# First terms copied into PSUM by ScalarE, and seven block products in one more down projection

## The chip, the cores and the metric

The kernel runs on one core of one Trainium2 chip. The metric is the device time of one launch in microseconds (us); the kernel before takes 1612.51 us as the median of three runs (1612.45 to 1613.25). One further execution was recorded by the hardware profiler, and every row shown is from that one. The engines are named as in the profile: PE is TensorE (its weight loads are PEld), DVE is VectorE, ACT is ScalarE, POOL is GpSimd, SP is SyncE, which here only issues DMAs. An engine works off its own queue in order. A matmul writes to one of eight PSUM banks of 128x512 fp32.

## The reference

Four layers work on an activation `x` of 2048 rows by 512 columns, with fp32 inputs and results. Layers 0 and 2 are Fourier mixings, layers 1 and 3 are GEGLU blocks; the two kinds share their weights:

```
z = layernorm(x)
mixing:  x = x + Cs @ (z @ Cd^T) - Ss @ (z @ Sd^T)          Cs, Ss 2048x2048; Cd, Sd 512x512
geglu:   x = x + (gelu(z @ w_gate) * (z @ w_up)) @ w_down    1792 hidden columns
```

## The kernel before, in words

**Three products for one.** Every fp32 operand is held as two tiles, a rounded part and the remainder (`split`, lines 145 to 149: ACT copies the rounded part, DVE subtracts it). `mm3` (lines 194 to 198) then makes one fp32 product of three matmuls over 512 columns, two with the rounded part of the left operand and one with its remainder.

**Seven products for eight.** Most large products are cut into two by two blocks, and seven block products are made in place of eight. Their operands are sums and differences of blocks, S1 to S4 on one side and T1 to T4 on the other; some block products share first terms, so that a sum that one of them left behind is added to the next.

**A mixing** works on four blocks `b` of 512 output rows. Its plan (lines 398 to 407) is: stage A11 for all four blocks, stage A12 for all four, and then for each block S2 (three interleaved sums: T2, T1 and T3), two groups of hidden products, S4, four groups, and two last groups. A11 leaves two tiles `sums[b]`, copied out of PSUM by ACT. A12 adds its own two banks to them on DVE (line 790) and puts `sums[b]` and the new sum away in HBM for blocks 1 to 3. S2 fetches both again; when the T2 banks are done, DVE adds `sums[b]` to them (`based`, line 753), and when T1 and T3 are done, DVE adds those too. The hidden products of a block collect in four banks over all eight groups, and at the end DVE adds the old rows of `x` to each bank (`x_add`, line 236) and POOL's queue writes them to HBM.

**A GEGLU layer** works on two halves `w` of 1024 rows. `up(n)`, n from 0 to 13, makes the gate and up products as seven block products; A11's result is copied out by ACT, and DVE adds A12's bank to it (`second`, line 1017). The down projection is of one of two kinds, by the table `SEVEN`. In its plain form (`down_steps`) 14 tiles of `w_down` are multiplied into four banks for each of two row parts. With an entry in `SEVEN`, pairs of tiles are multiplied as block products (`down_product`), half of them beside `up` and the rest behind it. Before the change three of the four GEGLU halves have an entry; the first half of layer 1 is plain.

**Who orders the work.** The program is written in order, and a scheduler of the language then places each instruction on its engine's queue by its own estimate of times. Two things bind it: `behind` (line 140), by which an instruction is not placed on its engine ahead of the last one there that read a PSUM bank (`bank_read`), from the S2 stage of the first mixing and throughout the second; and the pools of SBUF slots (94 tiles of 2 KB per partition) and PSUM banks, given out first in, first out. `queue` holds steps that are run one by one after a product, `slow` holds steps run at every ninth.

**The down projection's block pieces.** `weight_steps` (line 882) loads a pair of `w_down` tiles (three DMAs of 256, 128 and 128 KB), makes four half-width sums on DVE, splits four tiles and writes seven tiles of 256 KB to HBM through POOL's queue. In the kernel before, the seven pairs are made during `up` of the second half of layer 1.

Of the kernel before, what the change touches and what calls it, by code (L numbers as in the profile page):

```python
# [32 lines left out]
PACE = 9  # L33
SKEW = 2, 1
NSLOT = 94
SEVEN = {(1, 1): 7, (3, 0): 7, (3, 1): 5}
FORE = {0: 4, 2: 4}
MADE = 5
LEAD = 3
NK = NS // 2  # L40


@with_exitstack
def fnet_geglu(ctx: ExitStack, tc: tile.TileContext, x_in, ws, wh, wgu, wdn, wdc, out):
# [144 lines left out]
    def copied(src):  # L189
        v = sb.get()  # L190
        bank_read["ACT"] = nc.scalar.activation(v, src, AF.Copy)  # L191
        return v

    def mm3(ps, a, b, start, stop):
        (ah, al), (bh, bl) = a, b
        nc.tensor.matmul(ps, ah, bh, start=start, stop=False, skip_group_check=True)  # L196
        nc.tensor.matmul(ps, ah, bl, start=False, stop=False, skip_group_check=True)  # L197
        nc.tensor.matmul(ps, al, bh, start=False, stop=stop, skip_group_check=True)  # L198
# [46 lines left out]


    away = {}

# [230 lines left out]
    queue, slow, steps_done = [], [], [0]  # L479

    def step():
# [4 lines left out]
        steps_done[0] += 1  # L486
        if slow and steps_done[0] % PACE == 0:
            slow.pop(0)()
# [214 lines left out]
    def mix(layer):  # L703
# [14 lines left out]
        def hid_groups(b, groups):  # L718
# [9 lines left out]
            if last:  # L728
                xrows = [x_load(layer, b * NT + i) for i in range(NT)]
            for n, g in enumerate(groups):  # L730
                (hi, lo), w = take()
                for i in range(NT):
                    ts = slice(i * P, (i + 1) * P)
                    mm3(hid[b][i], (hi[:, ts], lo[:, ts]), w, first and n == 0, last and n == len(groups) - 1)
                sb.put(hi, lo, *w)
# [4 lines left out]
            if last:  # L740
                for i, ps in enumerate(hid.pop(b)):
                    x_add(layer, b * NT + i, xrows[i], ps)

# [8 lines left out]

        def based(b, c, ps):

            if b >= FORE[layer]:
                return copied(ps)
            v = sb.get()
            plus(v, sums[b][c], ps)
            return v

        def a11(b):
# [10 lines left out]
            sums[b] = [copied(p) for p in chain]  # L772
            if b < FORE[layer]:
                ps8.put(*chain)
            else:
                chains[b] = chain

        def a12(b):
            stream["more"] = 0
            if layer and b == 0:  # L780
                lend("x")
                lend("z")
            side = [ps8.get() for _ in range(2)]
            for k in range(NK):
                six(side, "B21", k, k == 0, k == NK - 1, "21" if b == NB - 1 else None)
            for c in range(2):
                v = sums[b][c]
                if b < FORE[layer]:
                    t = sb.get()
                    plus(t, v, side[c])  # L790
                    if b:
                        put_away((layer, b, c), v)
                        put_away((layer, b, c, "sum"), t)
                    else:
                        cs[0, c] = t
                else:
                    plus(v, v, side[c])
                    cs[0, c] = v
            ps8.put(*side)

        chains, sides, us, later = {}, {}, {}, {}

        def s2(b):
            last, fore = b == NB - 1, b < FORE[layer]
            if b == 0:
                lend("z")
                lend("x")
            if fore:
                chains[b] = [ps8.get() for _ in range(2)]
                if b:  # L810
                    sums[b] = [fetched((layer, b, c)) for c in range(2)]
                    cs.update({(0, c): fetched((layer, b, c, "sum")) for c in range(2)})
            chain, one, three = chains.pop(b), [ps8.get() for _ in range(2)], [ps8.get() for _ in range(2)]
            sides[b] = one, three
            if last:
                queue.extend([None] * 14 + [run for fetch in later.pop("fetches") for run in (None, fetch)])
            for i, k in skewed(3):
                if i == 0:
                    six(chain, "T2", k, fore and k == 0, k == NK - 1)
                elif i == 1:  # L820
# [5 lines left out]
                if i == 0:  # L826
                    us[b] = [based(b, c, p) for c, p in enumerate(chain)]
                    ps8.put(*chain)
                    if fore:
                        sb.put(*sums.pop(b))  # L830
                for c in range(2):
# [29 lines left out]
        for n, (b, what) in enumerate(plan(layer)):  # L861
            if n == len(plan(layer)) - 1:
# [10 lines left out]
        in_order[0] = False  # L873


# [48 lines left out]
    def down_weight_steps(k):  # L924
        return weight_steps(k, wdc, wdd)

    down_making = {}

# [26 lines left out]
    def geglu(w, layer):  # L955
# [55 lines left out]
        def first(n):  # L1011
            if n < NF:
                chain[n] = ps8.get()
                product(n, chain[n], "A11", "B11", True, True)
                c11[n] = copied(chain[n])

        def second(n):
            if n < NF:
                ps = ps8.get()
# [4 lines left out]
                finished(n, 0, 0, v)  # L1024
                sb.put(v)

        def up(n):
            if layer == 1 and w == 1:
                k, odd = divmod(n + 3, 2)
                if not odd and 2 <= k < NP:  # L1030
                    down_making[k] = down_weight_steps(k)
                    down_making[k][0]()
                if n % 2 == 0 and n // 2 + 1 in down_making:
                    queue.extend(down_making.pop(n // 2 + 1)[1])
            if n + 3 in making:
# [222 lines left out]
        if w == 0:  # L1258
            norms, others = block_steps(layer, 1)
            slow.extend(norms)  # L1260
            ahead_of_all = others[:ND] if layer in (3,) else []
        if not plain_down and layer == 1 or layer == 3:
# [18 lines left out]
        if w == 0:  # L1281
            queue.extend(([None] * 4 if ahead_of_all else []) + others[len(ahead_of_all):])
            if layer == 1:
                down_making.update((k, down_weight_steps(k)) for k in range(2))
                queue.extend([down_making[0][0], down_making[1][0], *down_making.pop(0)[1]])
        elif before_mix:
# [156 lines left out]
```

## Time and profile before

| what | value |
|---|---|
| median of three runs | 1612.51 us |
| span of the profiled execution, first to last instruction | 1611.3 us |
| what lies between the two | 1.2 us |
| PE busy | 1604.3 us (100%), 7050 matmul records |
| DVE, ACT, POOL busy | 1173.5, 819.9, 272.9 us |
| DMA | 424.67 MB, mean 264 GB/s |
| granted TensorE clock | 1.000 |

The profile's page counts for each engine how long it was busy, and follows one chain of waits back from the last instruction. A row of instructions names the line of the kernel, the engine, the operation, the tile written and the tiles read (s is an SBUF slot, p a PSUM bank, xwide and wide are slots lent from a larger tile, wb and wc are weight pieces in HBM), the shapes and the count; then the busy time, the mean duration of one, and the engine's idle time ahead of them with what ended it. Successive matmuls overlap, so the mean of 389 ns is one matmul's duration and not the distance between two.

### The profile page before, as it was taken

The page shows a single profiled execution, that of the slowest core. Times are in us where ns is not written, and L with a number is a line of the kernel's source. Part 1 is how long each engine was busy: PE and PEld are TensorE (multiplying, and loading weights), DVE is VectorE, ACT ScalarE, POOL GpSimd, SP SyncE. Part 2 cuts the span into 40 slices and gives each one's busy share as a digit, 9 for nine tenths or more (in the row PEclk, how much of TensorE's full clock was granted, in tenths as well). Part 3 has the DMA queues.
Part 4 walks back from the last instruction along what each step waited for, and adds up shares of the span by engine and source line. Part 5 has one row for each costly group of instructions (what it writes and reads, how often), then busy time and mean ns, then how long its engine had stood idle before and what let it go on. Part 6 is the DMA issues. An engine that isn't in the chain of part 4 may idle for free.

```text
span 1611.3 us, 22744 instructions
## 1 busy us (share of the span) xinstructions
PE 1604.3 (100%) x7050; PEld 1322.7 (82%) x7050; DVE 1173.5 (73%) x2025; ACT 819.9 (51%) x1566; POOL 272.9 (17%) x497
## 2 busy tenths in 40 slices
PE   9999999999999999999999999999999999999999
PEld 6888888888888888888888888888888888788887
DVE  7997888789867565666879978887864558844574
ACT  8744363535766434555756433644445535433360
POOL 4111010242545113220031000110400000010001
PEclk9999999999999999999999999999999999999999
DMA  9767786899978799986895776968989777796455
GB/s 358 266 232 256 248 304 220 281 304 326 348 274 297 223 351 322 369 297 231 283 304 184 245 256 196 318 210 307 274 280 276 244 218 217 233 301 203 148 179 157
DMA packets 250090, 424.67 MB, mean 264 GB/s; under 512 B 28848, under 2 KB 90032, under 8 KB 248944
## 3 DMA queue, kind: packets, MB, share of 16 engines
q1 hardware_dynamic: 223488, 334.33, 64.9%
q0 software_dynamic: 26480, 88.89, 15.2%
q8 instruction: 56, 0.92, 0.2%
q14 instruction: 66, 0.54, 0.1%
HBM read 339.48 MB, written 83.62 MB: 263 GB/s over the span
## 4 chain that ended last, share of the span: by engine, by line
PE 97%; DMA 1%; DVE 0%; POOL 0%; ACT 0%; issue 0%; SPq 0%; DVEq 0%; ACTq 0%; POOLq 0%
PE p L196 32%; PE p L197 32%; PE p L198 32%; DMA s<-wb 0%; DMA s<-t 0%; DMA s<-x 0%; DMA s<-ws 0%; DVE s L149 0%; DVE s L180 0%; ACT s L147 0%; POOL rstd L519 0%; SPq L224 0%; ACT s L556 0%; SPq L294 0%; POOL s L652 0%
## 5 line engine op out<-in xcount | busy, mean ns | idle before, releaser
L197 PE MATMUL p<-s,s 128*128 128x512 f32 x2334 | 905.7, 389 | 0.0
L198 PE MATMUL p<-s,s 128*128 128x512 f32 x2334 | 897.1, 389 | 0.0
L196 PE MATMUL p<-s,s 128*128 128x512 f32 x2334 | 866.6, 389 | 1.8 <-DMA s<-wb 1.3
L147 ACT ACTIVATE s<-s 128x512 fp32r<-128x512 f32 (+1 forms) x787 | 447.6, 606 | 333.9 <-PE p L198 59.0
L149 DVE TENSOR_TENSOR s<-s,s 128x512 fp32r<-128x512 f32 (+1 forms) x787 | 494.6, 662 | 93.6 <-ACT s L147 76.4
L196 PEld LDWEIGHTS p<-s,s 128*128 128x128 f32 x2334 | 437.9, 188 | 94.1 <-DMA s<-wb 1.7
L197 PEld LDWEIGHTS p<-s,s 128*128 128x128 f32 x2334 | 438.0, 188 | 92.2 <-DVE s L149 1.1
L198 PEld LDWEIGHTS p<-s,s 128*128 128x128 f32 x2334 | 438.1, 188 | 91.0
L184 DVE TENSOR_TENSOR s<-s,p 128x512 f32<-128x512 f32 x286 | 192.9, 683 | 212.8 <-PE p L198 124.9
L191 ACT ACTIVATE s<-p 128x512 f32<-128x512 f32 x218 | 127.9, 592 | 139.0 <-PE p L198 133.9
L180 DVE TENSOR_TENSOR s<-s,s 128x512 f32<-128x512 f32 (+1 forms) x323 | 193.3, 614 | 1.3
L952 ACT ACTIVATE s<-s 128x512 f32<-128x512 f32 x103 | 64.7, 629 | 74.9 <-DVE s L184 72.5
L147 ACT ACTIVATE s<-xwide 128x512 fp32r<-128x512 f32 x83 | 50.9, 622 | 68.0 <-PE p L197 17.6
L533 POOL TENSOR_SCALAR rstd<-rstd 128x1 f32<-128x1 f32 x40 | 20.5, 512 | 342.3 <-ACT s L532 335.9
L149 DVE TENSOR_TENSOR s<-xwide,s 128x512 fp32r<-128x512 f32 x83 | 56.4, 684 | 22.4 <-ACT s L147 22.0
L278 POOL DMA_DIRECT2D wb<-s x84 | 45.6, 545 | 57.1 <-ACT s L147 45.0
L530 ACT ACTIVATE s<-s 128x512 f32<-128x512 f32 x33 | 20.8, 629 | 67.6 <-PE p L198 32.8
L966 DVE TENSOR_TENSOR s<-s,s 128x512 f32<-128x512 f32 x75 | 51.7, 689 | 1.8
L556 ACT ACTIVATE s<-s,shift,rstd 128x512 f32<-128x512 f32 x56 | 45.3, 811 | 14.4 <-DVE shift L523 8.9
L187 DVE TENSOR_TENSOR s<-s,s 128x512 f32<-128x512 f32 (+1 forms) x67 | 39.6, 609 | 1.9 <-DMA s<-wgu 1.9
L240 POOL DMA_DIRECT2D x<-s x31 | 17.1, 551 | 140.8 <-DVE s L184 133.4
L184 DVE TENSOR_TENSOR xwide<-s,p 128x512 f32<-128x512 f32 x13 | 8.9, 688 | 43.1 <-PE p L198 43.1
(97 smaller groups left out, 560.9 us busy)
## 6 DMA issues: line engine op xcount, KB each, us to landing
s<-ws SPq DMA_DIRECT2D x384, 256.0 KB, 4.6
s<-wb SPq DMA_DIRECT2D x294, 256.0 KB, 5.1
s<-wc SPq DMA_DIRECT2D x133, 256.0 KB, 4.2
s<-wh SPq DMA_DIRECT2D x116, 256.0 KB, 5.1
wb<-s POOLq DMA_DIRECT2D x98, 256.0 KB, 4.4
s<-x SPq DMA_DIRECT2D x63, 256.0 KB, 5.4
xwide<-ws SPq DMA_DIRECT2D x52, 256.0 KB, 5.3
wc<-s POOLq DMA_DIRECT2D x49, 256.0 KB, 5.8
```

Source lines behind the costliest of these rows:

```text
L147: newest["ACT"] = nc.scalar.activation(hi, src, AF.Copy)
L149: newest["DVE"] = nc.vector.tensor_tensor(lo, src, f32(hi), op=ALU.subtract)
L180: nc.vector.tensor_tensor(out, a, b, op=ALU.subtract)
L184: bank_read["DVE"] = nc.vector.tensor_tensor(out, a, b, op=ALU.add)
L191: bank_read["ACT"] = nc.scalar.activation(v, src, AF.Copy)
L196: nc.tensor.matmul(ps, ah, bh, start=start, stop=False, skip_group_check=True)
L197: nc.tensor.matmul(ps, ah, bl, start=False, stop=False, skip_group_check=True)
L198: nc.tensor.matmul(ps, al, bh, start=False, stop=stop, skip_group_check=True)
L278: nc.gpsimd.dma_start(a, f32(t))
L556: nc.scalar.activation(z, x, AF.Identity, bias=shift, scale=rstd)
L952: nc.scalar.activation(t, g, AF.Gelu_apprx_tanh)
L966: nc.vector.tensor_tensor(t, t, v, op=ALU.mult)
```

## The change

Four things are changed together.

1. ACT copies a first term into a PSUM bank (`seed`), and the products then add to it, where they overwrote the bank before and DVE added the term afterwards. This is done for the A12 banks (seeded with `sums[b]`), the T2 banks of S2 (with `sums[b]`), the four hidden banks (with the rows of `x`, loaded at the start of S2), and A12's bank in `up` (with A11's bank). The results are copied out by ACT.
2. The first half of layer 1 gets an entry in `SEVEN`: seven block products over seven pairs of tiles, 294 matmuls in place of 336.
3. The pieces for it are made in the first mixing, a step at every fourth product from the S2 stage of block 0, and no longer in `up` of the second half of layer 1. The plain form's own pieces of `w_down` (14 tiles, 28 DMAs of 256 KB) are not written any more; the four plain tiles in the last half are loaded as they are and split when used.
4. The sums that S2 needs are fetched one group earlier, at the start of the last two groups of the block before. There are 98 slots in place of 94, and the space in which POOL's queue keeps its DMA descriptors is set to 8192 bytes.

```diff
-NSLOT = 94
-SEVEN = {(1, 1): 7, (3, 0): 7, (3, 1): 5}
+NSLOT = 98
+SEVEN = {(1, 0): 7, (1, 1): 7, (3, 0): 7, (3, 1): 5}
+DOWN_PACE = 4
...
+    def seed(ps, src):
+        inside = id(src) in ps8.held
+        with ExitStack() if inside else behind("ACT"):
+            i = nc.scalar.activation(ps, src, AF.Copy)
+        if inside:
+            bank_read["ACT"] = i
...
+    def x_seeded(b):
+        banks = [ps8.get() for _ in range(NT)]
+        for i, ps in enumerate(banks):
+            t = xrows.pop((b, i))
+            seed(ps, t)
+            sb.put(t)
+        return banks
+    def x_out(layer, i, ps):
+        t = copied(ps)
+        ps8.put(ps)
+        nc.gpsimd.dma_start(rows(layer + 1, i), t)
+        sb.put(t)
...
-                items.extend((F32R, halves(wds[f]), whole, NEAR[2]) for f in range(2 * SEVEN[layer + 1, w], NF))
+                items.extend((F32, (wdn[f],), plain, None) for f in range(2 * SEVEN[layer + 1, w], NF))
...
 hid_groups:
-                hid[b] = [ps8.get() for _ in range(NT)]
+                hid[b] = x_seeded(b)
...
+            if last and b + 1 < min(NB, FORE[layer]):
+                fetch_sums(b + 1)
...
 a12:
+            for c in range(2):
+                seed(side[c], sums[b][c])
+                if b:
+                    put_away((layer, b, c), sums[b][c])
             for k in range(NK):
-                six(side, "B21", k, k == 0, k == NK - 1, "21" if b == NB - 1 else None)
+                six(side, "B21", k, False, k == NK - 1, "21" if b == NB - 1 else None)
...
 s2:
+            for c in range(2):
+                seed(chain[c], sums[b][c])
...
-                    us[b] = [based(b, c, p) for c, p in enumerate(chain)]
+                    us[b] = [copied(p) for p in chain]
...
 mix:
+            if layer == 0 and (b, what) == (0, "S2"):
+                pace[0] = DOWN_PACE
+                for k in range(NP):
+                    load, making = down_weight_steps(k)
+                    slow.extend([load] + making)
...
 geglu:
-                c11[n] = copied(chain[n])
+                c11[n] = ps8.get()
+                seed(c11[n], chain[n])
...
-                product(n, ps, "A12", "B21", True, True)
-                v = c11.pop(n)
-                plus(v, v, ps)
+                ps = c11.pop(n)
+                product(n, ps, "A12", "B21", False, True)
...
-    nc = bacc.Bacc("TRN2", target_bir_lowering=False, num_devices=1)
+    nc = bacc.Bacc("TRN2", target_bir_lowering=False, num_devices=1, dynamic_dma_scratch_size=8192)
```

More of the change, by code (lines that the diff above doesn't have):

```diff
@@ L244, in x_add, with x_banks @@
             sb.put(t)
+    def x_banks(layer, b):
+        for i in range(NT):
+            xrows[b, i] = x_load(layer, b * NT + i)
+    def x_seeded(b):
[10 more added lines that the diff above has]
+        sb.put(t)
+    xrows = {}
     away = {}
@@ L486, in step @@
         steps_done[0] += 1
-        if slow and steps_done[0] % PACE == 0:
+        if slow and steps_done[0] % pace[0] == 0:
             slow.pop(0)()
@@ L733, in hid_groups @@
                     ts = slice(i * P, (i + 1) * P)
-                    mm3(hid[b][i], (hi[:, ts], lo[:, ts]), w, first and n == 0, last and n == len(groups) - 1)
+                    mm3(hid[b][i], (hi[:, ts], lo[:, ts]), w, False, last and n == len(groups) - 1)
                 sb.put(hi, lo, *w)
@@ L751, in six, with fetch_sums @@
             step()
[L753 to L759, printed above, removed]
+        def fetch_sums(b):
+            sums[b] = [fetched((layer, b, c)) for c in range(2)]
+            cs_next.update({(0, c): fetched((layer, b, c, "sum")) for c in range(2)})
+        cs_next = {}
         def a11(b):
@@ L807, in s2 @@
                 lend("x")
[L808 to L813, printed above, removed]
+            cs.update(cs_next)
+            cs_next.clear()
+            chain = [ps8.get() for _ in range(2)]
+            for c in range(2):
+                seed(chain[c], sums[b][c])
+            sb.put(*sums.pop(b))
+            x_banks(layer, b)
+            one, three = [ps8.get() for _ in range(2)], [ps8.get() for _ in range(2)]
             sides[b] = one, three
@@ L818, in s2 @@
                 if i == 0:
-                    six(chain, "T2", k, fore and k == 0, k == NK - 1)
+                    six(chain, "T2", k, False, k == NK - 1)
                 elif i == 1:
@@ L925, in down_weight_steps @@
         return weight_steps(k, wdc, wdd)
-    down_making = {}
     def piece_here(n, i, tiles):
```

49 lines of the change are left out of this document (12 added, 37 removed).

## The prediction

> **What bounds the kernel now.** I read the page first, then a table by stretches of time, PE's own waits, and the chain of waits in order of time.
>
> ```profile
> span 1611.3 us, 22744 instructions
> ...
> PE 1604.3 (100%) x7050; PEld 1322.7 (82%) x7050; DVE 1173.5 (73%) x2025; ACT 819.9 (51%) x1566; POOL 272.9 (17%) x497
> ...
> PE 97%; DMA 1%; DVE 0%; POOL 0%; ACT 0%; issue 0%; SPq 0%; DVEq 0%; ACTq 0%; POOLq 0%
> ```
> ```profile
> 300.00:400.00 100.00, 99.67 (x440) 82.22 (x439) 83.89 (x140) 50.28 (x93) 33.70 (x63) 1.00 0.93 308
> ...
> 600.00:700.00 100.00, 100.00 (x443) 82.77 (x442) 55.74 (x98) 50.84 (x113) 24.53 (x47) 1.00 1.01 341
> ...
> 800.00:900.00 100.00, 100.00 (x443) 82.80 (x442) 88.14 (x187) 60.24 (x114) 21.07 (x34) 1.00 0.77 255
> ...
> 1300.00:1400.00 100.00, 98.68 (x435) 81.17 (x434) 67.07 (x107) 52.11 (x91) 0.00 (x0) 1.00 0.68 212
> ```
> ```profile
> PE p L196 <- DMA s<-wb: 1.3, 1, 1.3
> PE p L196 <- ACT s L147: 0.3, 1, 0.3
> ```
>
> PE is the chain (97%). In the table the first counts are PE's and PEld's, then DVE, ACT and POOL with their busy time, the granted clock, the DMA share and GB/s. A stretch without a stall holds 443 products in 100 us, one per 225.7 ns, and that is so where DVE is busy 88% and where the DMAs run at 341 GB/s. Past the opening PE waits only twice: 0.3 us late in the first mixing and 1.3 us late in the first half of layer 3 (0.5 and 1.5 us over the pace, by the starts in rows below). So time can be won only by fewer products or by these few microseconds, and anything that stops PE is lost at once.
>
> **The change part by part.** *Fewer products.* Plain: 14 tiles x 2 row parts x 4 banks x 3 = 336 matmuls; block form: 7 products x 7 pairs x 2 banks x 3 = 294. The 42 that go are worth 42 x 225.7 ns = 9.5 us. With the waits above, the most that all of it can win is some 11.5 us.
>
> *The seeds and the copies.* The nearest rows for an ACT copy into a bank, its neighbours on ACT, and DVE's:
>
> ```profile
> L149 DVE TENSOR_TENSOR s<-s,s 128x512 fp32r<-128x512 f32 (+1 forms) x787 | 494.6, 662 | 93.6 <-ACT s L147 76.4 <-PE p L198 13.5 <-DMA wc<-s 0.9
> L147 ACT ACTIVATE s<-s 128x512 fp32r<-128x512 f32 (+1 forms) x787 | 447.6, 606 | 333.9 <-PE p L198 59.0 <-PE p L197 58.4 <-DMA s<-ws 48.3
> ...
> L184 DVE TENSOR_TENSOR s<-s,p 128x512 f32<-128x512 f32 x286 | 192.9, 683 | 212.8 <-PE p L198 124.9 <-ACT s L191 63.0 <-DMA s<-begun 12.1
> L191 ACT ACTIVATE s<-p 128x512 f32<-128x512 f32 x218 | 127.9, 592 | 139.0 <-PE p L198 133.9 <-DVE s L180 2.1 <-PE p L197 1.7
> ```
>
> No row shows a copy from SBUF to PSUM; the ends are 592 (bank read) and 606 ns (bank untouched), and I take 0.59. The built program has 145 more instructions on ACT and 66 fewer on DVE: 145 x 0.6 = 87 us brings ACT to some 907 us, 56%, and DVE loses some 45 us. Neither becomes the bound; DVE's relief is worth nothing, since the 88% stretch lost nothing. What counts is the order: a copy waits for the last product of its bank, and everything behind it on ACT waits too. The handover times:
>
> ```profile
> 1367.80 0.39 PE L197 MATMUL p<-s,s 128*128 128x512 f32 x1
> ...
> 1368.22 1.15 ACT L147 ACTIVATE s<-s 128x512 fp32r<-128x512 f32 x2 [1.71 <-PE p L197]
> ...
> 1370.66 2.50 DVE L149 TENSOR_TENSOR s<-s,s 128x512 fp32r<-128x512 f32 x4
> ```
> ```profile
> 376.59 0.61 PE L196 MATMUL p<-s,s 128*128 128x512 f32 x2
> ...
> 376.86 0.63 ACT L147 ACTIVATE s<-s 128x512 fp32r<-128x512 f32 x1 [3.00 <-DMA s<-ws]
> ...
> 377.54 0.73 PE L196 MATMUL p<-s,s 128*128 128x512 f32 x2 [0.33 <-ACT s L147]
> ```
>
> ACT starts 0.42 us after the start of the product it waits for, two ACT copies in a row take 1.15, four DVE subtractions 2.50 (0.60 each and 0.1 for the last), and PE starts 0.05 after ACT's end. I counted the places in the changed program's order.
>
> (a) A12 in the second mixing. There `behind` puts the two A12 seeds on ACT after the copies of the stage before, and the next product on PE is the first to use the seeded bank: no other work is ready between. From the start of the last product: 0.42 + 1.15 + 0.05 = 1.62 us to the next, where 0.23 is the pace: 1.4 us lost. Block 1 has a split between its copies, some 0.3 more. Four stages: 5.9 us. In the first mixing `behind` is off there and the seeds stand some 28 us ahead.
>
> (b) S4 of blocks 0 and 3 in the first mixing. Before, DVE read T2's banks, and PE filled the time with 22 hidden products that needed nothing but free banks. Now these products need seeds, which stand on ACT behind the two T2 copies and several splits; PE's next products are S4's, whose split stands behind the second copy. Its remainder stands on DVE behind an addition that needs that copy and two more instructions: 0.42 + 0.59 + 0.05 + 2.50 + 0.05 = 3.6 us, and the product that reads it is four places on (0.9 us): 2.7 us lost, twice, 5.4. Blocks 1 and 2 have other products between, and the second mixing 19 or more places at each of these seeds: nothing.
>
> (c) Shortly before, in block 3, a remainder stands behind six DVE instructions counted from a product nine places back, two of them half-width ones, of the moved pieces' making: 0.42 + 4 x 0.60 + 2 x 0.42 + 0.1 + 0.05 = 3.8, less 9 x 0.226 = 2.0: 1.8 us. It is the one place where the moved work costs PE by itself.
>
> (d) In `up` the seeded bank is first used 18 products (4.1 us) or more after A11's end, against one copy: nothing. Two copies late in the halves of layers 1 and 3 release a bank 0.4 us late each, and a split late in layer 1's second half is 1 us late: 1.8.
>
> *The moved making.* Per pair 512 KB in and 7 x 256 KB out, with seven pairs 16.5 MB, spread over 42 steps of four, 168 of the 192 products' steps (some 265 us): 62 GB/s more on 308 in the fullest stretch, 370, where 341 did without loss. What it takes from 600 to 760 us, and the 28 DMAs of plain pieces that go, gain nothing: no product waited there. Price 0 to 3 us, taken 0: loads for split items are issued nine or more microseconds ahead. POOL issues some 28 fewer; its descriptor space shows in no row, 0 to 1 us, taken 0. The fetch of the sums stands 10 to 30 us ahead of its seed, the rows of `x` more: nothing.
>
> *The end of a half with block products.* The next half's first gate piece is loaded by SP when a slot and its queue allow:
>
> ```profile
> 371.34 5.50 DMA s<-ws
> ...
> 1368.44 6.23 DMA s<-wb
> ```
> ```profile
> 1373.01 0.39 PE L198 MATMUL p<-s,s 128*128 128x512 f32 x1
> ...
> 1374.72 0.50 PE L196 MATMUL p<-s,s 128*128 128x512 f32 x1 [1.32 <-DMA s<-wb]
> ```
>
> That is the 1.3 us stall of the first half of layer 3 (1.71 from start to start, 1.5 over the pace), with the product 23 places (5.2 us) behind the last product that the load waits for. In the changed order it is 21 places (4.7 us), there and now also in the first half of layer 1: 2.0 us new and 0.5 more, 2.5.
>
> *The sum*, against the profiled execution, whose span lies 1.2 us under the median: -9.5 + 5.9 + 5.4 + 1.8 + 1.8 + 2.5 = +7.9 us; the old 0.5 us stall late in the first mixing may go. I take +7.5: 1620.
>
> **The rivals.** *All seeds hidden* (the other side): PE would have to find other products ahead of each seed, or the copies be short. The point is the sum of (a) to (d) and the load: below 9.5 us the change is faster. For it speaks that before, 218 ACT copies of banks cost PE nothing; against it that those had free banks and ready products behind them, and that (a) has none. At -9.5, and the 0.5: 1602.5. Its half-way case, (a) and the first S4 alone: -9.5 + 5.9 + 2.7 = -0.9, 1611.5. [...]
>
> *The DMAs become late* in the first mixing: at 370 GB/s against 341 for the 90 us of the fullest stretch, 8% or 7 us fall behind; loads 9 us ahead with 5.5 us landings have 3.5 us of cover, so 3.5 us reach PE in that stretch and perhaps as much again at the block's next loads: 1620 + 6 = 1626. For it speaks the share of 1.01 and the 0.5 us stall on `ws` already there; against it that 341 GB/s cost nothing elsewhere.
>
> *The clock falls*: if PE's waits made the throttle grant less, each of the three stretches of 2 to 3 us would slow the products that follow, at half rate some 15 of them (3.4 us): 5 us, 1625. The rows have the clock at 1.00 in every stretch, that of the 1.3 us wait too. [...]
>
> **How the numbers follow.** My sum 0.62, the late DMAs 0.12, the clock 0.03, the half-way case 0.15, all hidden 0.08. The range leaves out the last and, above, most of what DMAs and clock could add together: 1609 to 1627. A measurement of this kernel can tell about 0.2%, 3.2 us, from no change. Faster by more: 0.08 and a little of the half-way case, 0.09. Within: most of the half-way case and a low outcome of my sum, 0.17. Slower: 0.74.
>
> **What would show it.** PE's records should be 42 fewer, at 225.7 ns. PE's waits should name ACT's seeds: four of about 1.4 us between some 855 and 900 us (the A12 stages of the second mixing), and two groups of about 2.7 us in the first mixing, at some 130 and 360 us, on a split or DVE's remainder; and a DMA from `wb` near 570 us. DVE's busy time should be lower by about 45 us and ACT's higher by about 87. I am wrong if the stretches of 100 us in the first mixing and from 800 to 900 still hold 443 products; if they hold far fewer with ACT idle on DMAs, the late DMAs have it.

## The result and the profile after

| | before | after |
|---|---|---|
| median, measured side by side, four runs each | 1612.88 us (1612.45 to 1614.23) | 1638.45 us (1635.97 to 1639.21) |
| span of the profiled execution | 1611.3 us | 1634.0 us |
| PE's idle time between products, by their starts, past the opening | 2.6 us | 27.5 us |
| products at 0.43 us in place of 0.226, past the opening, in groups | none | 20, 4.0 us in all |
| from PE's last product to the end | 4.1 us | 6.7 us |

The ratio is 1.0158, 95% interval 1.0144 to 1.0173: slower by 1.6%, 25.6 us where 7.5 were forecast. The page of the profile after, and its table by stretches of 100 us (columns as in the prediction: PE, PEld, DVE, ACT, POOL, granted clock, DMA share, GB/s):

```profile
span 1634.0 us, 22639 instructions
PE 1605.1 (98%) x7008; PEld 1318.0 (81%) x7008; DVE 1135.9 (70%) x1958; ACT 888.8 (54%) x1711; POOL 269.3 (16%) x469
DMA 1%; issue 0%; DVE 0%; POOL 0%; POOLq 0%; DVEq 0%
```
```profile
200.00:300.00 100.00, 100.00 (x443) 82.81 (x442) 78.10 (x135) 63.19 (x132) 23.56 (x35) 1.00 0.90 310
300.00:400.00 100.00, 94.37 (x402) 75.77 (x401) 79.32 (x135) 55.40 (x105) 34.35 (x63) 0.98 0.92 308
...
600.00:700.00 100.00, 97.54 (x428) 79.76 (x428) 46.42 (x71) 44.22 (x98) 11.46 (x22) 1.00 0.93 271
700.00:800.00 100.00, 97.76 (x430) 80.13 (x429) 60.70 (x98) 55.05 (x102) 1.26 (x2) 1.00 0.61 196
800.00:900.00 100.00, 93.15 (x396) 75.89 (x395) 77.92 (x169) 59.76 (x115) 19.74 (x32) 0.97 0.69 228
...
1300.00:1400.00 100.00, 100.00 (x443) 82.84 (x442) 63.21 (x100) 52.47 (x97) 2.09 (x5) 1.00 0.73 223
```

The 42 products are gone and the pace is the old one: undisturbed stretches hold 443. But 300 to 400 us lacks 41 products, 800 to 900 lacks 47, and there the granted clock is below 1.00, as in no stretch of the profile before. The chain that the page follows back from the last instruction holds only the last 1% of the span, mostly DMAs, and no PE. ACT's busy time is 68.9 us higher, not 87, and DVE's 37.6 us lower, not 45. PE's own waits are nearly all on ACT:

```profile
PE p L205 <- ACT s L148: 9.0, 7, 2.6
PE p L205 <- ACT p L199: 8.0, 4, 4.1
PE p L206 <- DVE s L150: 2.4, 4, 1.3
PE p L205 <- ACT s L192: 1.7, 3, 1.2
```

(Line waited at, line waited for, us in all, times, longest. L199 is the seed, L192 a copy out of a bank, L148 and L150 the two halves of a split.) Three places show what the sum of the prediction did not have. The first A12 stage of the second mixing, PE and then ACT:

```profile
863.64 0.39 PE L206 MATMUL p<-s,s 128*128 128x512 f32 x1
863.86 0.39 PE L207 MATMUL p<-s,s 128*128 128x512 f32 x1
868.36 0.80 PE L205 MATMUL p<-s,s 128*128 128x512 f32 x1 [4.11 <-ACT p L199]
868.95 0.63 PE L206 MATMUL p<-s,s 128*128 128x512 f32 x1
869.38 0.63 PE L207 MATMUL p<-s,s 128*128 128x512 f32 x1
```
```profile
860.60 5.07 ACT L148 ACTIVATE s<-s 128x512 fp32r<-128x512 f32 x12
866.21 0.63 ACT L148 ACTIVATE s<-s 128x512 fp32r<-128x512 f32 x1 [0.54 <-DVE s L150]
866.75 1.07 ACT L192 ACTIVATE s<-p 128x512 f32<-128x512 f32 x2
867.70 1.12 ACT L199 ACTIVATE p<-s 128x512 f32<-128x512 f32 x2
```
```profile
868.00:872.50 4.50, 4.14 (x10) 3.31 (x11) 3.53 (x8) 2.18 (x5) 0.69 (x2) 0.50 0.64 192
```

The last product before the wait starts at 863.86, but ACT reaches the copies at 866.75 only: it works off 12 splits first, then stands 0.54 us for DVE and makes one more. After the wait the products come 0.43 us apart, and the stretch behind it has a granted clock of 0.50. Block 3 of the first mixing, PE, ACT's split that it waits for, and then the start and the end of DVE's rows:

```profile
356.54 0.73 PE L205 MATMUL p<-s,s 128*128 128x512 f32 x2 [2.57 <-ACT s L148]
```
```profile
355.86 1.90 ACT L148 ACTIVATE s<-s 128x512 fp32r<-128x512 f32 x3 [0.86 <-DVE s L188]
```
```profile
345.53 3.10 DVE L150 TENSOR_TENSOR s<-s,s 128x512 fp32r<-128x512 f32 x5
348.54 0.69 DVE L188 TENSOR_TENSOR s<-xwide,s 128x512 f32<-128x512 f32 x1
...
353.20 0.42 DVE L188 TENSOR_TENSOR s<-s,s 128x256 f32<-128x256 f32 x1
353.53 0.75 DVE L181 TENSOR_TENSOR s<-s,s 128x256 f32<-128x256 f32 x2
...
355.14 0.69 DVE L188 TENSOR_TENSOR s<-s,s 128x512 f32<-128x512 f32 x1
...
356.94 0.69 DVE L150 TENSOR_TENSOR s<-s,s 128x512 fp32r<-128x512 f32 x1
```

None of these DVE rows has an idle time ahead of it: DVE works without a pause from 345.5 to 357.6. The split of 355.86 waits for DVE's sum of 355.14, and the moved making (the 128x256 rows) stands ahead of that sum. Last, ACT in the second half of layer 1:

```profile
647.49 0.63 ACT L561 ACTIVATE s<-s 128x512 f32<-128x512 f32 x1 [5.18 <-DMA s<-x]
```

It stands 5.2 us for a row of `x`, for norm statistics taken ahead for layer 2, and then works off the statistics of several rows with what PE needs among them; PE waits 3.2 us in all from 652 to 657 us. In the kernel before, ACT is idle for 13.0 us ahead of the same step (at 610.42 us) and PE loses nothing there, so an idle ACT alone does not stop PE.

### The profile page after: what moved, and what is told of

Its sections match the earlier page's. It is cut to its first block, busy times and chain, and to the rows that moved or that the text cites. A ratio compares the mean times of both kernels' runs of the same rounds, so it can differ in the third digit from the quotient of the medians.

```text
span 1634.0 us, 22639 instructions
## 1 busy us (share of the span) xinstructions
PE 1605.1 (98%) x7008; PEld 1318.0 (81%) x7008; DVE 1135.9 (70%) x1958; ACT 888.8 (54%) x1711; POOL 269.3 (16%) x469
## 5 line engine op out<-in xcount | busy, mean ns | idle before, releaser
L150 DVE TENSOR_TENSOR s<-s,s 128x512 fp32r<-128x512 f32 (+1 forms) x806 | 507.7, 665 | 127.8 <-ACT s L148 108.7
L148 ACT ACTIVATE s<-s 128x512 fp32r<-128x512 f32 (+1 forms) x806 | 452.4, 606 | 222.6 <-DVE s L181 63.9
L185 DVE TENSOR_TENSOR s<-s,p 128x512 f32<-128x512 f32 x196 | 132.6, 683 | 205.8 <-PE p L207 163.7
L181 DVE TENSOR_TENSOR s<-s,s 128x512 f32<-128x512 f32 (+1 forms) x364 | 217.9, 615 | 5.4 <-DMA s<-ws 3.0
L192 ACT ACTIVATE s<-p 128x512 f32<-128x512 f32 x233 | 133.9, 593 | 114.5 <-PE p L207 112.0
L980 ACT ACTIVATE s<-s 128x512 f32<-128x512 f32 x84 | 52.8, 630 | 71.5 <-DVE s L185 70.8
L564 POOL TENSOR_SCALAR rstd<-rstd 128x1 f32<-128x1 f32 x40 | 30.6, 764 | 281.1 <-ACT s L563 266.2
L148 ACT ACTIVATE s<-xwide 128x512 fp32r<-128x512 f32 x73 | 44.7, 625 | 49.7 <-DVE xwide L185 25.9
L994 DVE TENSOR_TENSOR s<-s,p 128x512 f32<-128x512 f32 x56 | 38.4, 685 | 34.6 <-PE p L207 31.7
L980 ACT ACTIVATE s<-p 128x512 f32<-128x512 f32 x28 | 16.7, 598 | 76.3 <-PE p L207 72.5
L150 DVE TENSOR_TENSOR s<-xwide,s 128x512 fp32r<-128x512 f32 x73 | 49.6, 688 | 10.9 <-ACT s L148 10.0
L188 DVE TENSOR_TENSOR s<-s,s 128x512 f32<-128x512 f32 (+1 forms) x72 | 43.5, 610 | 17.2 <-DMA s<-ws 15.9
L199 ACT ACTIVATE p<-p 128x512 f32<-128x512 f32 x56 | 32.7, 584 | 36.4 <-PE p L207 27.6
L669 DVE STREAM_TRANSPOSE wide<-s 128x512 f32<-128x512 f32 x27 | 19.1, 709 | 36.3 <-ACT s L587 36.3
```

The source lines that it names most:

```text
L148: newest["ACT"] = nc.scalar.activation(hi, src, AF.Copy)
L150: newest["DVE"] = nc.vector.tensor_tensor(lo, src, f32(hi), op=ALU.subtract)
L181: nc.vector.tensor_tensor(out, a, b, op=ALU.subtract)
L185: bank_read["DVE"] = nc.vector.tensor_tensor(out, a, b, op=ALU.add)
L188: nc.vector.tensor_tensor(out, a, b, op=ALU.add)
L980: nc.scalar.activation(t, g, AF.Gelu_apprx_tanh)
```

## The experiments

All times stand against the kernel before, run on the same chip (1612.4 to 1613.0 us).

**1. The A12 seeds freed.**

```diff
-        with ExitStack() if inside else behind("ACT"):
+        with ExitStack() if inside or free else behind("ACT"):
...
-                seed(side[c], sums[b][c])
+                seed(side[c], sums[b][c], True)
```

> The changed kernel, with the A12 seeds no longer held behind the copies of the stage before, so that ACT may take them as soon as their sources and banks are there; the same instructions otherwise. Theory A (it is the place of the seeds on ACT that stops PE): the four waits of 4.3, 1.8, 1.5 and 1.5 us between 860 and 900 us go, and the 2.7 us of products at 0.43 us each behind the first of them go too, since the granted clock falls only after the long wait: 9.0 + 2.7 = 11.7 us off 1638.4, about 1627; the stretch from 800 to 900 holds 440 or more products at a clock of 1.00. Rival B (it is ACT's backlog of splits there): the splits stay, so waits on ACT of 3 us or more stay in that stretch and the time is above 1634. Rival C (the clock falls by itself, whatever PE waits for): the waits go and the products at 0.43 us stay, about 1629.5.

Measured: 1623.58 us, ratio 1.0068 (1.0053 to 1.0083). The four waits and the slow products behind them are gone, as its table by stretches shows (columns as above):

```profile
800.00:900.00 100.00, 100.00 (x443) 82.82 (x442) 83.40 (x178) 65.83 (x126) 19.58 (x34) 1.00 0.78 260
```

ACT does more in that stretch than before the edit (65.8 against 59.8 us busy), so its backlog alone stops nothing; the order behind the copies does. Between the two profiled executions 11.4 us are won (1634.0 to 1622.6). That this is so near the expected 11.7 is in part luck: PE's idle time falls by 9.6 us and the end by 1.2, but the 13 slow products that go are made up by 12 new ones at block 0 and in block 3 (19 in place of 20 in all). The medians lie 14.9 apart.

**2. The hidden banks opened by a product again.**

```diff
-                hid[b] = x_seeded(b)
+                hid[b] = [ps8.get() for _ in range(NT)]
...
-                    x_out(layer, b * NT + i, ps)
+                    x_add(layer, b * NT + i, xrows.pop((b, i)), ps)
```

> The changed kernel, with the hidden banks opened by a product again and the rows of x added on DVE at the end of a block, as before; the other seeds stay. Theory A (the hidden products that PE used to fill its waits with now stand behind seeds on ACT): the 2.9 us at S4 of block 0 in the first mixing go wholly; at block 3 the 2.7 us at S4 go, and with them the 1.8 us of slow products, while the remainder behind the copies of T2 may cost up to 2.9 us a little later: 2.9 + 2.7 + 1.8 - 2.9 = 4.5 us off, 1634, and up to 1631 if that remainder is in time. Rival B (the moved making and its loads on DVE and the DMA queues cause the waits in block 3): block 0 gains its 2.9, block 3 none: 1635.5. Rival C (both waits are those of the splits behind the copies and would stay without the seeds): 1638.

Measured: 1636.39 us, 1.0140 (1.0124 to 1.0157). The wait at block 0's S4 goes wholly, which shows term (b) there. Block 3 gets worse: 300 to 400 us holds 376 products, with 2.4, 1.9 and 3.9 us of waits, the last of them on a load (3.4 us on `wh`), and 19 slow products; that costs about what is won at block 0. The edit gives DVE its additions back, but it also loads the rows of `x` later, so which of the two does it is not shown.

**3. No seed at all; the block products and the moved making stay.** Every first term is added by DVE as before the change.

```diff
-                seed(side[c], sums[b][c])
...
-                t = copied(side[c])
+                plus(t, sums[b][c], side[c])
```

> The changed kernel without any seed: every first term is added by DVE as in the kernel before; the w_down products of the first half by seven block products, the making moved into the first mixing and the early fetch of the sums stay. Theory A (the seeds are most of the loss): no wait on a seed, 9.5 us fewer products; the moved making alone costs what block 3 shows, 3.5 us there and no clock drop, and the 2.6 us of the end: 1612.9 - 9.5 + 3.5 + 2.6 = 1609.5. Rival B (the moved making on DVE needs the relief that the seeds give it): with the additions back, DVE has 19 instructions or more ahead of remainders in block 3, by the built order 7.8 us at its worst place, and 3.2 us late in layer 1, with slow products behind the long wait: 1612.9 - 9.5 + 7.8 + 1.8 + 3.2 + 2.6 = 1618.8 or more.

Measured: 1639.39 us, 1.0171 (1.0149 to 1.0193): as slow as the whole change. Rival B holds in kind, with 36 us of loss beside the 9.5 won where it had some 15. In the profiled execution, the slowest of the four, waits and slow products take some 22 us in the first mixing, 18 from 640 to 810 us, and 4 elsewhere. The list of PE's waits in this kernel:

```profile
PE p L210 <- DVE s L154: 15.3, 11, 3.7
PE p L209 <- ACT s L196: 5.3, 2, 4.5
PE p L209 <- ACT s L152: 3.0, 3, 1.4
```

DVE's remainders (L154) lead, with waits in all four blocks of the first mixing and late in layer 1.

**4. The A12 seeds free, the hidden banks unseeded, and the making at every third step.**

```diff
-DOWN_PACE = 4
+DOWN_PACE = 3
```

> The changed kernel with three edits: the A12 seeds free on ACT, the hidden banks unseeded, and the moved making spread over every third step in place of every fourth, so that it ends before block 3. Theory A (the three causes are apart and add up): 11.7 us from A12, 2.9 from block 0, 1.25 + 3.5 + 2.7 + 1.8 = 9.2 from block 3, less about 1.5 us that the built order shows as tight in block 2: 1638.4 - 11.7 - 2.9 - 9.2 + 1.5 = 1616; what is left over 1612.9 - 9.5 = 1603.4 are the waits late in layer 1 (3.3 + 2.1 + 0.9 + 0.5 + 0.5) and the end (2.6). Rival B (a faster making brings the loads together and makes the DMAs late in blocks 1 and 2): waits on DMA or on splits that wait for DMA appear between 200 and 330 us, 5 us or more: 1621 or more.

Measured: 1616.83 us, 1.0025 (1.0015 to 1.0035), theory A's 1616. Together the three edits take 21.6 of the 25.6 us; PE waits 13.2 us in this profile, and no product is slow. The parts fit less well than the sum: between 280 and 360 us PE still waits some 5.5 us, where 1.5 were expected.

**5. The seeds alone, without the block products and without the moved making.** The slots (94) and the descriptor space are those of the kernel before, too.

```diff
-SEVEN = {(1, 0): 7, (1, 1): 7, (3, 0): 7, (3, 1): 5}
+SEVEN = {(1, 1): 7, (3, 0): 7, (3, 1): 5}
...
-                for k in range(NP):
-                    load, making = down_weight_steps(k)
-                    slow.extend([load] + making)
```

> The kernel before with all the seeds and the copies that go with them, and without the rest: the first half's w_down products stay plain, the making of the pieces stays where it was. Theory A (the two parts overlap: without the seeds the moved making overfills DVE, 36 us of waits in e3; without the moved making the seeds cost only their own places): the four A12 stages 9 us, S4 of block 3 some 2.7 us, a remainder late in layer 1 some 3 us, no wait at 340 to 358 us and none near 655: 1612.9 + 9 + 2.7 + 1.8 + 3 = 1629, that is 1625 to 1633. Rival B (seeds and moved making add up, and the seeds cost what after and e3 differ by, less than nothing): 1612. Rival C (the long wait of 4.3 us at the first A12 needs the moved making's slots or loads): four waits of 1.4 there and no slow products, 1624 or less.

Measured: 1642.38 us, 1.0183 (1.0167 to 1.0198). Every theory missed the size: the wait at the first A12 is 8.8 us here. In the timeline of ACT it stands for a load, in a split that is ahead of the copies (L191) and seeds:

```profile
864.78 3.41 ACT L147 ACTIVATE s<-s 128x512 fp32r<-128x512 f32 x8
872.01 0.63 ACT L147 ACTIVATE s<-s 128x512 fp32r<-128x512 f32 x1 [3.81 <-DMA s<-ws]
872.54 0.58 ACT L191 ACTIVATE s<-p 128x512 f32<-128x512 f32 x1
```

So the price of a seed held behind others was here that of everything queued ahead of it, the 3.8 us for a late load included. With experiment 3 this gives four cells: neither part 1612.9, seeds alone 1642.4, block products and making alone 1639.4, both 1638.4. Were the parts independent, both would take 1612.9 + 29.5 + 26.5 = 1669; 30 us of waits fall in the same places or are relieved by the other part, and how much each of these makes is not separated. The slots and the descriptor space were not tried by themselves.

**6. The making at every third step, alone**, on the kernel after.

```diff
-DOWN_PACE = 4
+DOWN_PACE = 3
```

> The changed kernel with one number changed: a step of the moved making on every third step in place of every fourth, so that the making ends before block 3's last stages. Theory A (block 3's waits of 1.25 and 3.5 us come from the making's instructions on DVE and its loads): both go, the S4 wait there becomes short, since by the built order ACT's copies have 11 fewer places behind them; new waits of 1 to 1.5 us in block 2. 1638.4 - 4.7 - 2.7 - 1.8 + 2 = 1631. Rival B (the waits in block 3 are those of the seeds, wherever the making stands): 1636 to 1639, with the same waits between 344 and 370 us. Rival C (the faster making makes loads late in blocks 0 to 2): 1640 or more.

Measured: 1629.21 us, 1.0100 (1.0084 to 1.0115), theory A's 1631. The waits of 1.25 and 3.4 us in block 3 are gone and one of 1.3 us in block 1 is new: the two came from where the making stood. At block 3's S4 only 0.9 us are left.

**7. Three more edits of the order, on top of experiment 4.**

```diff
+            if layer == 1:
+                slow.extend([lambda: None] * 3)
             slow.extend((lambda k=k: terms_ahead(layer + 1, k, NK)) for k in range(NK))
...
+            queue.extend([None] * 4)
             queue.extend((lambda k=k: first_rows(layer + 1, k)) for k in range(NK))
...
-            at = {i: begun_load(i) for i in range(NT)}
+            at = {i: begun_load(i) for i in range(2 * NT)}
```

> The fourth experiment's kernel (free A12 seeds, hidden banks unseeded, every third step) with three more edits of the order alone: the norm statistics ahead for layer 2 start three entries of their slow list later in layer 1's second half; the norms of layer 2's first rows start four queue entries later; and the eight loads of the begun rows at the very end take their tiles together, not four after the first rows are stored. Theory A (the wait near 655 us stands behind statistics that wait on ACT for rows of x which the block form writes only at its end; the wait near 780 stands behind norms crowded onto ACT and DVE; the end waits for tiles that stores hold): 2.9 us near 655, 2.7 and 0.8 us late in layer 1, and 2 us of the end go: 1616.8 - 8.4 = 1608.5, under the kernel before. Rival B (ACT and DVE are simply full there, and the waits move to the next place): 1614 to 1617, with waits of the same sum between 650 and 810 us. Rival C (the end is set by the write and read of the begun rows): 2 us of it stay, 1610.5.

Measured: 1612.19 us, 1.0001 (0.9992 to 1.0010). Late in layer 1 PE no longer waits (2.1 and 0.7 us in experiment 4), near 655 us 0.6 us is left of 2.9, and from the last product to the end it is 4.5 us, not 6.1. The chain of waits at the end of the kernel after shows why; the loads of the begun rows stand behind the store of the first finished ones, which holds their tiles:

```profile
1619.37 3.25 DMA out<-s
1622.62 1.05 POOL s L1238 x2
1623.67 0.35 issue
1624.02 4.33 DMA s<-begun
```

The median fell by 4.6 us, not by theory A's 8.4: between 280 and 360 us and near 855 us the waits stayed.

**8. A pause in the making, and the hidden banks of the second mixing seeded.**

```diff
-                    slow.extend([load] + making)
+                    slow.extend([load] + making + [lambda: None] * (3 if k == 4 else 0))
...
-                hid[b] = [ps8.get() for _ in range(NT)]
+                hid[b] = x_seeded(b) if layer else [ps8.get() for _ in range(NT)]
```

> The seventh experiment's kernel with two more edits of the order: three empty entries in the slow list behind the making of the fifth pair, so that no making falls on block 2's S2 and S4 stages and the rest still ends before block 3's end; and the hidden banks of the second mixing seeded again (in the first they stay opened by a product). Theory A (what is left between 280 and 360 us, 0.6 + 0.5 + 0.5 + 0.8 + 1.0 + 1.9 = 5.3 us over the pace, stands behind the making's instructions on DVE and ACT): 4 to 5 us of it go, and the 1.7 us near 855 us, where the additions of x that the seeds replace stand, go too: 1612.2 - 4.5 - 1.5 = 1606, 0.4% under the kernel before. Rival B (those waits are late loads, which the same bytes in the same time keep): 1611 to 1612, with waits on DMA or on splits behind it in the first mixing.

Measured: 1610.42 us, 0.9986 (0.9976 to 0.9995), with single times from 1606.6 to 1614.7. Between 280 and 360 us 2.0 us are left of 5.6; near 855 us 1.4 of 1.7. The median lies between the two theories. In the profiled run 3.6 us came back near 645 us, with six slow products.

**9. The edits of the order without any seed**: experiment 3 with the pace, the pause and the three edits of experiment 7.

```diff
-DOWN_PACE = 4
+DOWN_PACE = 3
...
-                    slow.extend([load] + making)
+                    slow.extend([load] + making + [lambda: None] * (3 if k == 4 else 0))
```

> The third experiment's kernel (no seed anywhere) with the edits of the order alone: a step of the making on every third step with the pause behind the fifth pair, the later norm statistics and norms, the loads of the begun rows together. Theory A (seven block products lost their gain to the order of the moved making and of the norms, not to DVE's load): by the built order its worst places are 1.6, 1.0, 0.5 and 1.9 us: 1612.9 - 9.5 + 5 = 1608, and up to 1612. Rival B (DVE needs the relief of the seeds: it is some 45 us busier than in the changed kernel): waits on DVE's remainders of 2 to 4 us stay in blocks 0, 1 and 3, and in layer 1, with slow products behind those over 2.5 us: 1620 or more.

Measured: 1620.81 us, 1.0050 (1.0038 to 1.0062), rival B's time, though no wait is longer than 1.6 us and none is followed by slow products. The order gives 18.6 us back, and 10 us lie between this and experiment 8, which differs by the seeds alone. So the seeds are worth something to this form of the kernel. Why is shown in part: between the two profiled executions, 5.7 us apart, PE's waits on DVE's remainders differ by 3.2 us (4.6 against 1.4) and those on loads by 2.3 (3.0 against 0.7), and those on ACT hardly (4.6 against 4.4).

**10 and 11. The row that ACT stands for.** Experiment 10 moves the statistics by one entry (and the norms of the first rows by two, the other way), experiment 11 makes the load of their first row an entry of its own.

```diff
-                slow.extend([lambda: None] * 3)
+                slow.extend([lambda: None] * 4)
```

> The eighth experiment's kernel with two numbers changed: the norm statistics ahead for layer 2 start four entries of their slow list later, not three, and the norms of the first rows two queue entries later, not four. Theory A (in the eighth experiment ACT stood 7.4 us at 632 to 640 us for the first of these rows, and PE lost 3.6 us and six slow products behind it; how late the rows are differs from run to run, so its times spread from 1606.6 to 1614.7): ACT no longer waits there, the 3.6 and 1.4 us go, the times lie closer together, and the median comes to 1606 to 1608. Rival B (the rows are late by more than an entry, 12 us): the wait stays, 1609 to 1611. Rival C (the spread has another cause): no wait near 655 us in the profile, and a median of 1609 to 1611 with the same spread.

Measured: 1617.82 us, 1.0020 (1.0008 to 1.0032). Theory A fell. In the timeline of ACT the wait has moved with the entry, at its old length:

```profile
650.29 0.63 ACT L565 ACTIVATE s<-s 128x512 f32<-128x512 f32 x1 [7.62 <-DMA s<-x]
```

```diff
-        if i == 0:
+        if "terms" not in fresh:
             fresh["terms"] = x_load(layer, 0)
...
-                slow.extend([lambda: None] * 3)
+                slow.extend([lambda: None] * 3 + [lambda: fresh.update(terms=x_load(layer + 1, 0))] + [lambda: None])
```

> The eighth experiment's kernel with the load of the first row for the norm statistics as an entry of its own, two entries (some 24 us of steps) ahead of the statistics that read it; the statistics start two entries later than there, the norms of the first rows one queue entry earlier. In the eighth and the tenth experiment the load was issued at 631.6 and at 643.6 us and ACT stood 7.4 and 7.6 us for it, whichever entry it had. Theory A (the load and its reader are issued in one step, so ACT waits the load's 7 us wherever the step stands): with the load ahead ACT does not stand there, PE's 3 to 4 us near 650 us and the slow products go, and the median comes to 1605 to 1608, with less spread than 1606.6 to 1614.7. Rival B (the queue that issues the load is what is late, and it holds the load back to its reader anyway): a wait of 4 us or more on ACT stays and the median is 1610 to 1617.

Measured: 1606.85 us, 0.9973 (0.9962 to 0.9983), faster than the kernel before. The load is issued at 632.76 us, the statistics run at 654 and wait for a product, not for the row; PE waits nowhere near. From the timelines of SP and ACT, and the table by stretches:

```profile
632.76 0.32 SPq L237 DMA_DIRECT2D s<-x  x1
```
```profile
654.25 0.63 ACT L565 ACTIVATE s<-s 128x512 f32<-128x512 f32 x1 [0.55 <-PE p L210]
```
```profile
600.00:700.00 100.00, 100.00 (x443) 82.81 (x442) 46.81 (x72) 38.32 (x73) 8.47 (x14) 1.00 0.90 264
```

PE waits 3.7 us in this run, 1.1 more than before the change, and the end takes 5.8 us, 1.7 more; with the 9.5 us of the products that makes -6.7, and the span is 7.1 us shorter (1604.2 against 1611.3).

## Why the prediction was wrong

The direction was right, slower with products won and waits lost; the sum was too small by 18 us (1638.45 against 1620, outside the range). Against the profiled executions, 22.7 us apart:

| step | forecast | measured |
|---|---|---|
| 42 products | -9.5 | -9.5 |
| (a) four A12 stages | 5.9 | 4.3 + 0.4 + 1.7 + 1.4 + 1.3 = 9.1 |
| (b) S4 of blocks 0 and 3 | 5.4 | 2.7 + 2.5 = 5.2 |
| (c) block 3 shortly before | 1.8 | 3.4, and 1.25 ten us earlier |
| (d) late copies and a split | 1.8 | 0.5 + 0.5 + 1.85 + 0.85 + 0.35 = 4.1 |
| load at the end of a half | 2.5 | 0 |
| the two old waits | -0.5 | -2.0 |
| clock | 0 | 20 slow products, 4.0 |
| statistics near 652 us | no term | 3.2 |
| the end | no term | 2.6 |

The measured column gives 21.3 of the 22.7.

**The step that failed most is the first stage of (a).** "From the start of the last product: 0.42 + 1.15 + 0.05" took ACT to be free when the product ended. At three of the four stages it was, and the waits of 1.3 to 1.7 us fit the 1.4 forecast. At the first, ACT came 2.9 us after that product's start: priced at 1.4 us, the stage cost 4.7, and 13 of the 20 slow products (2.6 us) follow it, together 5.9 of the 13.9 us between the columns. Experiment 1 shows that it is the order and not ACT's load; experiment 5, with 8.8 us at the same place, that the price of such an order can be twice as high with other work ahead. The seed itself takes what was taken for it: 592 ns is its mean (57 copies from SBUF; 584 from a bank), 0.59 the forecast. The 606 ns taken for a copy that leaves the banks alone mixed half-width ones in (409 ns); those of 128x512 alone take 625, so with a bank at one end (592 ns written, 593 read) a copy is some 33 ns shorter here.

**(b) held**, in size and place. Experiment 2 takes its first half away with the seeds; the second half is not the seeds' alone, since experiment 6, which moves only the making, leaves 0.9 of it. **(c)** had the right cause, instructions of the making ahead on DVE, and half the size: I counted six instructions ahead of a remainder, where DVE worked for 12 us without a pause, and PE's wait was mainly for the rounded part that ACT copies from DVE's late sum (2.57 us), only 0.41 us for a remainder. Experiment 6 shows that the making stood in the way. That it is "the one place where the moved work costs PE by itself" was wrong: with the making moved and no seeds, some 22 us are lost in all four blocks of the first mixing (experiment 3). "DVE's relief is worth nothing, since the 88% stretch lost nothing" is the sentence refuted, by the 10 us between experiments 8 and 9: the average of 88% said nothing on instructions that come in bursts. DVE was busy only 74% of the span in experiment 9, and the seeds were still worth those 10 us to it. To the change as it stood they were worth less: with the block products and the making in place the seeds brought 1 us (1639.4 to 1638.4), and alone they cost 29.5.

**The load from `wb`** did not come: no wait on a DMA stands in PE's list after, and the old 1.3 us is gone too. Why the load came in time is not shown.

**The clock** was the rival with 0.03. The waits were forecast at 2 to 3 us, and the rows of the kernel before have the clock at 1.00, that of the wait of 1.3 us too; none of them shows the half rate that the rival is priced with. The kernel after shows it, a granted clock of 0.50 with products 0.43 us apart. Between the opening and PE's last product the granted clock of the thirteen profiles falls to 0.50 in 19 places, each time for 3.41, 6.83 or 10.24 us (in the kernel after from 369.40 us for 3.41 and from 867.75 us for 6.83), and in each profile all its changes lie on one grid of 3.41 us. In these profiles the falls go with how few products start within one step of this grid, and not with how long a wait is. A step without a wait holds 15 products. Counted by starts, a step at full clock with five products or fewer was followed by half rate each time (18 times), one with eight or more never, and one with six or seven once in 13 times. In the kernel after the steps ahead of its two falls hold five products (from 365.99 us, with waits of 1.21 and 0.83 us) and none (from 864.34 us), and the wait of 2.57 us at 356.54 us is followed by no fall; so the 2.5 us that experiment 9's rival B sets for a wait with slow products behind it are no limit here. Steps of the kernel after, and then of experiment 1 (columns as above):

```profile
352.34:355.75 3.41, 1.63 (x8) 1.01 (x6) 3.41 (x9) 0.63 (x1) 1.09 (x2) 1.00 1.05 293
355.75:359.16 3.41, 2.21 (x8) 1.53 (x9) 3.41 (x7) 2.42 (x4) 1.32 (x3) 1.00 1.06 333
864.34:867.75 3.41, 0.00 (x0) 0.00 (x0) 3.41 (x10) 2.87 (x7) 0.13 (x1) 1.00 0.14 54
867.75:871.16 3.41, 2.80 (x7) 2.25 (x8) 3.41 (x8) 1.71 (x4) 0.94 (x2) 0.50 0.66 220
```
```profile
354.10:357.51 3.41, 0.85 (x5) 0.38 (x3) 3.41 (x9) 1.37 (x3) 1.17 (x3) 1.00 1.07 284
357.51:360.93 3.42, 3.42 (x8) 2.27 (x9) 3.42 (x7) 1.67 (x3) 2.30 (x5) 0.50 1.04 289
```

(The counts in brackets are of products that overlap a step, up to two more than start in it.) The same wait in block 3, 2.96 us from start to start in the kernel after and 2.95 in experiment 1, is cut in two by the grid in the first and costs no clock, and lies within one step in the second and costs four slow products. Likewise the two waits at block 0's S4 (1.42 and 1.67 us in both) cost no clock in the kernel after and six slow products in experiment 1. So whether a wait of 2 to 3 us makes the clock fall is partly luck here. The price is small and near the rival's 5 us: 0.20 us for a product, 4.0 in the kernel after.

**Two terms were missing.** The statistics for layer 2 read a row right behind its load, and ACT, in order, stands for it; a split and a copy that PE needs stand behind that (5.2 us of ACT, 3.2 of PE). I priced only what the changed half itself does. Experiments 10 and 11 show that ACT waits for the load's landing wherever the step is (7.6 us in experiment 10, 7.4 in experiment 8), and that the load as an earlier step takes the wait away (0.55 us in experiment 11, for a product); why the same step costs PE nothing in the kernel before stays open. The end is set by loads and stores that I did not compare at all; experiment 7 takes 1.6 us of it off. Of the rivals, late DMAs do not stand in PE's list of waits after, and the half-way and all-hidden cases did not come.

## What to carry to other kernels

ACT's queue charged the seeds of the first A12 stage with everything ahead of them, 4.3 us of PE's time in the kernel after and 8.8 in experiment 5: price a copy that must follow another by where that engine stands at that moment, with its latest load, not by the copy's own handover time. When work is moved, look at each place's bursts and at who reads the results of the new form and when; busy shares of 84 and 88%, read before the change, said nothing of the 22 us that the first mixing lost without the seeds. And before a change is given up, try the order of its steps: here eight edits, all but one of order and pace, turned +25.6 us into -5.8 with the same products.

## What the runs showed that was not expected

In the kernel after, two waits of PE of 1.21 and 0.83 us that end within one step of 3.41 us were followed by a granted clock of 0.50, as was every step at full clock with five products or fewer in the thirteen profiles, and averages over 100 us show no more of it than 0.95 to 0.98. A load and its first reader issued in one step cost ACT 5.2, 7.4 and 7.6 us in the kernel after and in experiments 8 and 10; with the load two steps ahead the wait is gone. And the times of kernels with such a wait spread by 8 us (1606.6 to 1614.7, 1610.7 to 1618.9), those of the kernel before by 4 at most; that the place of the waits on the grid makes this spread is likely, and not shown. In experiment 11 six of eight times lie within 1.1 us, and two at 1609.8 and 1612.8; what those two lost was not seen, since the profile shows one of the fast ones. In the first mixing, where experiments 10 and 11 have the same order, PE lost 5.3 us between 325 and 350 us in the one profile and 2.3 in the other; why is open.
